# Block-diagonal tiles and runs of 1024 bytes in the token stage of a two-path attention kernel, and gradient rows that are scaled where they are used

## The chip, the cores and the metric

The kernel runs on one core of a Trainium2 chip. The metric is the device time of one execution in microseconds; the median of the runs counts. Matrix products are in bf16 with sums in f32.

## The reference

The forward function mixes two attention paths by a gate; the kernel computes its output and, for a given `grad_out`, the gradients of eleven of its inputs.

```python
def A(x, wq, wk, wv, wo):             # S=2048, D=576, 32 heads of 18, one shared k and v
    p = softmax(scores(x @ wq, x @ wk) * 18 ** -0.5)
    return heads(p @ (x @ wv)) @ wo
def B(x, mem0, Wq, Wk, Wv, Wo):       # 32 heads of 128, 64 segments of 32 tokens
    mem = mem0                        # 8 memory rows
    for s in range(64):
        h = concat([mem, x[:, 32 * s:32 * s + 32]])
        q, k, v = h @ Wq, h @ Wk, h @ Wv          # per head
        p = softmax(where(mask, q @ k.T * 128 ** -0.5, -1e9))
        o = (p @ v) @ Wo
        mem = o[:, :8]; outs.append(o[:, 8:])
    return concat(outs)
g = sigmoid((x * gate_w).sum(-1))
out = g * A(x, ...) + (1 - g) * B(x, ...)
grads = vjp(out)(grad_out)
```

Path B is the second path. Its gradient starts from the rows `(1 - g) * grad_out`, called db in the kernel, with `1 - g` in `omg_all`.

## The kernel before

The program is one sequence of stages on one core. A preparation (0 to about 111 us) projects path A's queries, transposes inputs and scales the gradient rows. Then come a projection stage for path B, the chain of segments forward (woven with path A's first pass), **the token stage** `b_bulk`, the chain backward (woven with path A's second pass), `b_post`, and the weight gradients `b_dw`.

**The token stage.** In the chain only the 8 memory rows of each segment have been attended; here the 2048 tokens of path B are. The work is 128 groups: 16 token tiles of 128 tokens (four segments of 32) by 8 groups of four heads. The loop `for t in range(NG + 9)` runs one *tick* per group, software-pipelined: `order` lists the stages of a tick with their delays in ticks, and each engine executes its part of that list in the order in which it is written. A tick holds, in this order:

- `st_QT`, `st_KT`: TensorE transposes four heads of q, then of k, into a PSUM tile `x_tr`; VectorE copies 128x512 of it to `x_qT`, `x_kT` (L836). Each *rides* one more 128x128 transpose in the fifth place of the same PSUM tile: that of the memory part of dS (with q) and of P (with k) of an older group. VectorE copies the ridden 128x128 (L822) into columns 128 to 255 of a tile `x_DT` or `x_PT`, and fills columns 0 to 127 by its own 32x32 stream transpose of the token part (L823).
- `st_OT`, `st_VT`, `st_GT`: the same for o, v and dO. ScalarE copies o (`x_oT`) and v, VectorE copies dO (`x_dOT`). GpSimd multiplies `x_prod = x_dOT * x_oT` (L938).
- `st_B`, in four parts in between: the products of o with the output weights.
- `st_Om`, `st_Qm`: one 128x512 matmul each, of the memory rows (a block-diagonal `x_vmB` or `x_kmB`) with columns 128 to 255 of `x_PT` or `x_DT`, into a PSUM tile `x_po`.
- `st_SDm`, `st_SDx`: scores and dP. ScalarE takes the exponential `x_E`; VectorE forms `x_dS` (L897).
- `st_R`, `st_M`: VectorE's row sum `x_l`, reciprocal `x_r` and mask on `x_E` (L904); GpSimd's product `x_P` (L915).
- `st_K`, every second tick: gradients of the memory rows' k and v.
- `st_Ox`, `st_Qx`: the token part of o and dq. A token attends its own segment only, so each of four heads needs four 32x32 blocks of P: `attend_x` issues 16 matmuls in 32x32 tiles of the array, which add to `x_po`. ScalarE copies the result to `x_o` or `x_dq`.

Tiles of 128x2048 (16 heads of one token tile, a *chunk* of four ticks) are loaded and stored by SP's queue: `x_q`, `x_k`, `x_v`, `x_dO` in, `x_o` and `x_dq` out, each partition in one run of 4096 bytes.

**The gradient rows.** In the preparation, a loop of 20 steps u multiplies path A's output weights and the gate-scaled rows (`product`), and beside it `scale_go` (L1739, VectorE) forms db for token tile u+1 one step ahead, GpSimd copies its last columns to `xtail` (L1846), TensorE transposes it, and every fourth step `keep_rows` (L1743) stores four tiles to `db_dram` by GpSimd's DMA queue. `put` evacuates a product to a tile `a_QDs` (L82 on VectorE, L84 on ScalarE; eight buffers) and stores it to `qs_dram` in turn by SP's and GpSimd's queues. An earlier loop of 20 steps does the same for the queries, with `scale_go` into `xtok`. In `b_post`, whose loop over t has VectorE copies `y_T` (L1405) in each step, `load_h` reads `db_dram` back at t = 31 as `w_h` for the weight gradients.

Of the kernel before, what the change touches and what calls it, by code (L numbers as in the profile page):

```python
# [51 lines left out]
class Kern:  # L52
# [52 lines left out]
    def setup_B_dram(self, dram):  # L105
# [4 lines left out]
        self.db_dram = t("db_dram", [T, D])  # L110
# [617 lines left out]
    def b_bulk(self, wp, lp, sp, psum):  # L728
# [3 lines left out]
        mB = {w: [wp.tile([P, 4, 4, E], BF16, name=f"x_{w}mB{i}") for i in range(2)] for w in ("k", "v")}  # L732
        mT = {}
        C = {}
        NG = NTT * 8
        NC = NTT * 2

        def load(c, names):
# [4 lines left out]
            for w in names:  # L743
# [12 lines left out]
                else:  # L756
                    d[w] = lp.tile([P, 16, P], BF16, name=f"x_{w}", bufs=BQ if w in deep else 3)
                    nc.sync.dma_start(d[w][:].rearrange("p h e -> p (h e)"),
                                      self.xtok[w][tt * P:(tt + 1) * P, h0 * P:h0 * P + 2048])
# [16 lines left out]
        def store(t, dst, src):  # L776
            if t % 4 == 3:
                tt, h0 = t // 8, 16 * (t // 4 % 2)
                due[1].append((dst[tt * P:(tt + 1) * P, h0 * P:h0 * P + 2048], src[:].rearrange("p h e -> p (h e)")))
# [11 lines left out]
        def transp(d, r, nm, pt):  # L791
            self.tr(pt[:, 4, :], d[:, 1, r, :].rearrange("p i t -> p (i t)"), P)
            o = sp.tile([P, 256], BF16, name=nm, bufs=2)
            return o, d[:, 0, r, :].rearrange("p i t -> p (i t)")

        def attend_m(PT, m):
            po = psum.tile([P, 4, P], F32, name="x_po", bufs=2)
            self.mm(po[:].rearrange("p i e -> p (i e)"), lhsT=PT[:, 128:256], rhs=m.rearrange("p i e -> p (i e)"),
# [3 lines left out]
        def attend_x(o, po, PT, v):  # L802
            for i in range(4):
                for c in range(4):
                    r32 = slice(32 * c, 32 * c + 32)
                    self.mm(po[r32, i, :], lhsT=PT[r32, 32 * i:32 * i + 32], rhs=v[r32, i, :],
                            start=False, stop=True, tp=(32 * c, 32 * c))
            nc.scalar.copy(o, po[:])
# [3 lines left out]
        def trans(t, w, nb, ride=None):  # L812
            pt = psum.tile([P, 5, P], BF16, name="x_tr", bufs=2)
            if 0 <= t < NG:
                tt, g, r, d = view(t)
                for i in range(4):
                    self.tr(pt[:, i, :], d[w][:, 4 * (g % 4) + i, :], P)
            o2 = ride and ride(pt)
            if 0 <= t < NG:
                trans_out(t, w, nb, pt)  # L820
            if o2:
                nc.vector.tensor_copy(o2[0][:, 128:256], pt[:, 4, :])  # L822
                nc.vector.transpose(o2[0][:, 0:128], o2[1])  # L823

        def trans_out(t, w, nb, pt):
            tt, g, r, d = view(t)
            if w == "v":
                o = chunk(t, "vT", [P, 4, 16, SEG], 2)
# [6 lines left out]
            o = sp.tile([P, 4, P], BF16, name=f"x_{w}T", bufs=nb)  # L835
            nc.vector.tensor_copy(o[:], pt[:, 0:4, :])  # L836
            sc[w + "T", t] = o

        def ride(t, nm, out):
            def put(pt):  # L840
                if 0 <= t < NG:
                    tt, g, r, d = view(t)
                    o2 = transp(d[nm], r, "x_" + out, pt)
                    sc[out, t] = o2[0]
                    return o2
# [73 lines left out]
        def st_Om(t):  # L919
            tt, g, r, d = view(t)  # L920
            sc["po", t] = attend_m(sc["PT", t], mB["v"][t // 4 % 2][:, g % 4])

        def st_Ox(t):
            tt, g, r, d = view(t)
            o = chunk(t, "o", [P, 16, P], 2)
            attend_x(o[:, r, :], sc.pop(("po", t)), sc.pop(("PT", t)), d["v"][:, r, :])
            store(t, self.xtok["o"], o)

        def st_OT(t):
            tt, g, r, d = view(t)  # L930
            pt = psum.tile([P, 5, P], BF16, name="x_tr", bufs=2)
            for i in range(4):
                self.tr(pt[:, i, :], d["o"][:, 4 * (g % 4) + i, :], P)
# [24 lines left out]
        def st_Qm(t):  # L958
            tt, g, r, d = view(t)
            sc["pq", t] = attend_m(sc["DT", t], mB["k"][t // 4 % 2][:, g % 4])  # L960

        def st_Qx(t):
            tt, g, r, d = view(t)
            dq = chunk(t, "dq", [P, 16, P], 2)
            attend_x(dq[:, r, :], sc.pop(("pq", t)), sc.pop(("DT", t)), d["k"][:, r, :])
# [4 lines left out]
        def st_K(t):  # L970
# [4 lines left out]
            for a in range(2):  # L975
                for i in range(4):
                    r32 = slice(32 * i, 32 * i + 32)
                    h = 4 * (g % 4 - 1 + a) + i
                    self.mm(pk[r32, a, 0, :], lhsT=d["dS"][:, 1, h, :], rhs=d["q"][:, h, :], tp=(0, 32 * i))
# [1403 lines left out]
```

## Time and profile before

| | |
|---|---|
| median of 3 runs | 5270.73 us (5256.26 to 5274.28) |
| profiled execution | 5275.43 us, span 5273.7 us |
| TensorE / VectorE / ScalarE / GpSimd busy | 95% / 67% / 62% / 41% of the span |
| mean granted TensorE clock | 0.988 |
| DMA over the span | 959.23 MB, 182 GB/s |
| token stage, first and last tick's start | 2045.41 and 2644.76 us |

A row of the timeline gives the start and the duration in us, the engine, the source line, the operation with output <- input, the shape, the count, and in brackets the idle time of the engine before it with what released it. PE is TensorE, PEld its weight loads, DVE VectorE, ACT ScalarE, POOL GpSimd, SP SyncE. A row of the waits gives the waiting engine, its tile and line, the releaser, then the total in us, the times and the longest. "issue" as a releaser is time in which the engine waited for nothing that the profile shows. A row of a DMA queue gives packets, MB and the time that its packets took as a share of 16 engines' time. A row of groups gives the count, the busy time and the mean of one in ns. A row of a source line or tile gives count, shortest/median/longest in ns, and the first and last start.

### The profile page before, as it was taken

What the parts mean: (1) busy time and instruction counts of PE and PEld (TensorE: products, weight loads), DVE (VectorE), ACT (ScalarE), POOL (GpSimd) and SP (SyncE); (2) the same over time, 40 slices, a digit from 0 to 9 for tenths busy, and PEclk for the clock granted to TensorE, in tenths of its full rate; (3) what the DMA queues carried; (4) which work ended last, traced back from release to release, by engine and by line L of the source; (5) the groups of instructions that cost most, each with busy time, mean ns of one, the idle gap of its engine ahead of it and who ended that gap; (6) DMA issues with size and microseconds to landing.
All of it is one profiled execution on the core that took longest, in us unless ns stands there. A gap on an engine that the chain in (4) does not pass through costs nothing. (4 is left out here: it accounts for less than half of the span.)

```text
span 5273.7 us, 216258 instructions
## 1 busy us (share of the span) xinstructions
PE 5025.2 (95%) x92973; PEld 2779.6 (53%) x93152; DVE 3526.8 (67%) x7041; ACT 3272.5 (62%) x4701; POOL 2166.9 (41%) x4164
## 2 busy tenths in 40 slices
PE   8999999999999998988889999999999999999999
PEld 5444444444444445666655555555555577754445
DVE  4348888888888887666657778788888841333332
ACT  4237888888888886555557777777777732222211
POOL 3015666665655655333323444444444421111213
PEclk9999999999999999999999999999999999999999
DMA  8855676656765456888885788878888787965654
GB/s 273 266 149 133 140 137 143 138 138 138 144 137 127 116 111 176 260 258 253 241 282 159 175 183 181 177 179 180 181 182 177 169 198 213 267 217 187 189 165 138
DMA packets 1070902, 959.23 MB, mean 182 GB/s; under 512 B 618245, under 2 KB 926413, under 8 KB 1059956
## 3 DMA queue, kind: packets, MB, share of 16 engines
q1 hardware_dynamic: 958556, 695.16, 54.7%
q0 software_dynamic: 102032, 240.46, 15.1%
q8 instruction: 728, 11.93, 1.0%
q10 hardware_dynamic: 9352, 9.77, 0.6%
q14 instruction: 234, 1.92, 0.1%
HBM read 518.26 MB, written 375.52 MB: 169 GB/s over the span
## 5 line engine op out<-in xcount | busy, mean ns | idle before, releaser
L2098 DVE TENSOR_TENSOR b_dS<-b_dP,b_E 128x512 bf16<-128x512 f32 x2048 | 1317.5, 685 | 559.9 <-PE b_dP L87 253.6
L1933 DVE TENSOR_TENSOR a_W<-a_dP,a_E 128x512 bf16<-128x512 f32 x2048 | 1313.8, 683 | 227.9 <-issue 103.6
L2047 ACT ACTIVATE b_E<-b_S 128x1024 bf16<-128x1024 f32 x1024 | 1049.2, 1025 | 608.5 <-PE b_dP L87 491.0
L1902 ACT ACTIVATE a_E<-a_S 128x1024 bf16<-128x1024 f32 x1024 | 1050.0, 1025 | 244.5 <-PE a_dP L87 163.6
L87 PE MATMUL a_acc<-a_E,l_VK 128*32 128x512 bf16 x4096 | 594.5, 385 | 7.8 <-issue 2.8
L87 PE MATMUL r_pj<-WT,r_dT 128*32 128x288 bf16 x12288 | 489.3, 290 | 8.9 <-issue 4.6
L87 PE MATMUL w_acc<-w_d,w_h 128*128 128x512 bf16 (+1 forms) x2342 | 480.0, 380 | 3.7 <-issue 1.1
L87 PEld LDWEIGHTS <-b_QS 32*128 32x128 bf16 (+1 forms) x8192 | 238.6, 91 | 439.9 <-issue 394.1
L87 PE MATMUL b_S<-b_KV,b_QS 32*128 32x512 bf16 x2048 | 404.7, 386 | 36.1 <-ACT b_E L2047 21.2
L87 PE MATMUL a_S<-a_QD,l_KV 32*128 32x512 bf16 x2048 | 398.7, 383 | 40.7 <-ACT a_E L1902 39.1
L87 PE MATMUL b_dP<-b_KV,b_QS 32*128 32x512 bf16 x2048 | 404.0, 389 | 3.1 <-DVE b_dS L2098 1.7
L87 PE MATMUL a_acc<-a_W,l_WK 128*32 128x512 bf16 x2048 | 405.5, 390 | 0.3 <-DVE a_W L1933 0.2
L87 PE MATMUL b_acc<-b_dS,b_QS 128*18 128x512 bf16 x2048 | 398.7, 384 | 1.8 <-issue 1.2
L87 PE MATMUL b_acc<-b_E,b_QS 128*18 128x512 bf16 x2048 | 397.6, 384 | 0.8 <-issue 0.8
L87 PE MATMUL a_dP<-a_QD,l_KV 32*128 32x512 bf16 x2048 | 398.2, 385 | 0.0
L87 PEld LDWEIGHTS <-hm 128*32 128x32 bf16 x7680 | 263.8, 96 | 196.8 <-issue 15.0
L87 PEld LDWEIGHTS <-r_dT 128*32 128x32 bf16 x12288 | 277.1, 96 | 135.5 <-issue 87.2
L87 PEld LDWEIGHTS <-w_h 128*128 128x128 bf16 (+1 forms) x2528 | 214.5, 100 | 245.2 <-issue 17.7
L938 POOL TENSOR_TENSOR x_prod<-x_dOT,x_oT 128x512 bf16<-128x512 bf16 x128 | 148.0, 1156 | 299.5 <-ACT x_oT L935 282.5
L87 PEld LDWEIGHTS <-l_KV 32*128 32x128 bf16 x4096 | 123.8, 91 | 250.5 <-issue 210.1
L87 PEld LDWEIGHTS <-l_WK 128*32 128x32 bf16 x2048 | 98.9, 93 | 218.7 <-issue 218.7
L87 PE MATMUL x_b<-WoN,x_oT 128*128 128x288 bf16 x1024 | 211.0, 290 | 1.2 <-issue 1.2
(475 smaller groups left out, 10114.0 us busy)
## 6 DMA issues: line engine op xcount, KB each, us to landing
b_QS<-qs_dram SPq DMA_DIRECT2D x233, 200.0 KB
dOx_dram<-p_tok SPq DMA_DIRECT2D x16, 1024.0 KB
c_vx<-vx_dram SPq DMA_DIRECT2D x64, 256.0 KB
krow_dram<-c_k POOLq DMA_DIRECT2D x64, 256.0 KB
qrow_dram<-c_q POOLq DMA_DIRECT2D x64, 256.0 KB
vrow_dram<-c_v POOLq DMA_DIRECT2D x64, 256.0 KB
x_q<-qx_dram SPq DMA_DIRECT2D x32, 512.0 KB
x_dO<-dOx_dram SPq DMA_DIRECT2D x32, 512.0 KB
```

What stands on the lines that cost most here:

```text
L87: return self.nc.tensor.matmul(out, lhsT, rhs, start=start, stop=stop, tile_position=tp, skip_group_check=True)
L938: nc.gpsimd.tensor_tensor(out=sc["prod", t][:], in0=sc["dOT", t][:], in1=oT[:], op=ALU.mult)
L1902: nc.scalar.activation(E_[n][:], S.pop(n)[:], ACT.Exp, scale=SCALEA)
L1933: nc.vector.tensor_tensor(out=W_[n][:, i, :], in0=dP[i][:], in1=E_[n][:, i, :], op=ALU.mult)
L2047: nc.scalar.activation(E_[n][:], S.pop(n)[:], ACT.Exp, scale=SCALEA)
L2098: nc.vector.tensor_tensor(out=D_[n][:, i, :], in0=dP[i][:], in1=E_[n][:, i, :], op=ALU.mult)
```

## The change

- **Token stage.** The chunk tiles become `[P, 4, 528]` with 512 of each 528 columns used, so that a partition's 4096 bytes lie in four pieces of 1024 bytes, and its DMA goes in runs of that size. The ridden transpose is copied together with q or k (128x640, one VectorE copy) and used from that tile. The stream transpose goes to a tile of its own, which is spread to a block-diagonal `[P, 4, 4, 32]` tile: for P by four VectorE copies of 32x128 into one of two tiles that are zeroed once, for dS by one GpSimd product of 128x512 with the mask `bmask`. `attend_x` then issues 4 matmuls of 128x128 instead of 16 of 32x32.
- **Gradient rows.** `db_dram` and its stores go. `load_h` reads `grad_out`, and 16 VectorE products in `b_post` (t = 32 to 47, one in each step) scale it in place.
- **Preparation.** `a_QDs` has twelve buffers instead of eight, and both loops scale two tiles ahead instead of one.

```diff
@@ -107,7 +107,6 @@
         t = lambda nm, sh, dt=BF16: dram.tile(sh, dt, name=nm)
         self.xT_dram = t("xT_dram", [NKT, P, T])
         self.dbT_dram = t("dbT_dram", [NKT, P, T])
-        self.db_dram = t("db_dram", [T, D])
         self.da_dram = t("da_dram", [T, D])
         self.dxB_dram = t("dxB_dram", [T, D])
         self.st_WoT = t("st_WoT", [4, P, J])
@@ -730,10 +729,12 @@
         NTT = self.NTT
         mx = self.maskX
         mB = {w: [wp.tile([P, 4, 4, E], BF16, name=f"x_{w}mB{i}") for i in range(2)] for w in ("k", "v")}
+        diag = [wp.tile([P, 4, 4, SEG], BF16, name=f"x_PTd{i}") for i in range(2)]
         mT = {}
         C = {}
         NG = NTT * 8
         NC = NTT * 2
+        pieces = lambda t: t[:, :, 0:512].rearrange("p g (i e) -> p g i e", e=E)
 
         def load(c, names):
             if c >= NC:
@@ -754,9 +755,10 @@
                             self.mtok[w[0]][tt * 32:(tt + 1) * 32, h0 * P:h0 * P + 2048]
                             .rearrange("r (g i e) -> r g i e", i=4, e=E)[:, :, i, :])
                 else:
-                    d[w] = lp.tile([P, 16, P], BF16, name=f"x_{w}", bufs=BQ if w in deep else 3)
-                    nc.sync.dma_start(d[w][:].rearrange("p h e -> p (h e)"),
-                                      self.xtok[w][tt * P:(tt + 1) * P, h0 * P:h0 * P + 2048])
+                    t = lp.tile([P, 4, 528], BF16, name=f"x_{w}", bufs=BQ if w in deep else 3)
+                    d[w] = pieces(t)
+                    nc.sync.dma_start(t[:, :, 0:512], self.xtok[w][tt * P:(tt + 1) * P, h0 * P:h0 * P + 2048]
+                                      .rearrange("p (g x) -> p g x", x=512))
 
         after = {4: ("vB",), 5: ("v",), 6: ("mT",), 7: ("q", "dO"), 9: ("k", "kB")}
         deep = ("q", "dO", "k")
@@ -776,7 +778,8 @@
         def store(t, dst, src):
             if t % 4 == 3:
                 tt, h0 = t // 8, 16 * (t // 4 % 2)
-                due[1].append((dst[tt * P:(tt + 1) * P, h0 * P:h0 * P + 2048], src[:].rearrange("p h e -> p (h e)")))
+                due[1].append((dst[tt * P:(tt + 1) * P, h0 * P:h0 * P + 2048].rearrange("p (g x) -> p g x", x=512),
+                               src[:, :, 0:512]))
 
         def store_pd(t, w, src):
             if t % 4 == 3:
@@ -788,23 +791,32 @@
                 (nc.scalar if end else nc.sync).dma_start(dst, src)
             due.append([])
 
-        def transp(d, r, nm, pt):
+        def transp(d, r, pt):
             self.tr(pt[:, 4, :], d[:, 1, r, :].rearrange("p i t -> p (i t)"), P)
-            o = sp.tile([P, 256], BF16, name=nm, bufs=2)
-            return o, d[:, 0, r, :].rearrange("p i t -> p (i t)")
+
+        def block_diag(d, r, t, nm):
+            o = sp.tile([P, 4, SEG], BF16, name=f"x_{nm}", bufs=2)
+            nc.vector.transpose(o[:].rearrange("p i q -> p (i q)"), d[:, 0, r, :].rearrange("p i t -> p (i t)"))
+            if nm == "PT":
+                full = diag[t % 2]
+                for c in range(4):
+                    r32 = slice(32 * c, 32 * c + 32)
+                    nc.vector.tensor_copy(full[r32, :, c, :], o[r32])
+            else:
+                full = sp.tile([P, 4, 4, SEG], BF16, name="x_DTd", bufs=2)
+                nc.gpsimd.tensor_tensor(out=full[:], in0=o[:].unsqueeze(2).to_broadcast([P, 4, 4, SEG]), op=ALU.mult,
+                                        in1=self.bmask[:, :, 0:1].unsqueeze(1).to_broadcast([P, 4, 4, SEG]))
+            sc[nm, t] = full
 
         def attend_m(PT, m):
             po = psum.tile([P, 4, P], F32, name="x_po", bufs=2)
-            self.mm(po[:].rearrange("p i e -> p (i e)"), lhsT=PT[:, 128:256], rhs=m.rearrange("p i e -> p (i e)"),
+            self.mm(po[:].rearrange("p i e -> p (i e)"), lhsT=PT, rhs=m.rearrange("p i e -> p (i e)"),
                     start=True, stop=False)
             return po
 
         def attend_x(o, po, PT, v):
             for i in range(4):
-                for c in range(4):
-                    r32 = slice(32 * c, 32 * c + 32)
-                    self.mm(po[r32, i, :], lhsT=PT[r32, 32 * i:32 * i + 32], rhs=v[r32, i, :],
-                            start=False, stop=True, tp=(32 * c, 32 * c))
+                self.mm(po[:, i, :], lhsT=PT[:, i].rearrange("p c q -> p (c q)"), rhs=v[:, i, :], start=False, stop=True)
             nc.scalar.copy(o, po[:])
 
         sc = {}
@@ -814,17 +826,12 @@
             if 0 <= t < NG:
                 tt, g, r, d = view(t)
                 for i in range(4):
-                    self.tr(pt[:, i, :], d[w][:, 4 * (g % 4) + i, :], P)
-            o2 = ride and ride(pt)
-            if 0 <= t < NG:
-                trans_out(t, w, nb, pt)
-            if o2:
-                nc.vector.tensor_copy(o2[0][:, 128:256], pt[:, 4, :])
-                nc.vector.transpose(o2[0][:, 0:128], o2[1])
-
-        def trans_out(t, w, nb, pt):
-            tt, g, r, d = view(t)
+                    self.tr(pt[:, i, :], d[w][:, g % 4, i, :], P)
+            trans_out(t, w, nb, pt, ride and ride(pt))
+
+        def trans_out(t, w, nb, pt, rode):
             if w == "v":
+                tt, g, r, d = view(t)
                 o = chunk(t, "vT", [P, 4, 16, SEG], 2)
                 nc.scalar.copy(o[:, :, r, :].rearrange("p s h t -> p h s t"),
                                pt[:, 0:4, :].rearrange("p h (s t) -> p h s t", t=SEG))
@@ -832,17 +839,21 @@
                     for c in range(4):
                         due[1].append((self.vT_dram[4 * tt + c][:, 16 * (t // 4 % 2):16 * (t // 4 % 2) + 16, :], o[:, c]))
                 return
-            o = sp.tile([P, 4, P], BF16, name=f"x_{w}T", bufs=nb)
-            nc.vector.tensor_copy(o[:], pt[:, 0:4, :])
-            sc[w + "T", t] = o
+            lo, hi = 0 if 0 <= t < NG else 4, 5 if rode else 4
+            if lo < hi:
+                o = sp.tile([P, 4 if w == "dO" else 5, P], BF16, name=f"x_{w}T", bufs=nb)
+                nc.vector.tensor_copy(o[:, lo:hi, :], pt[:, lo:hi, :])
+                if lo == 0:
+                    sc[w + "T", t] = o
+                if rode:
+                    rode(o[:, 4, :])
 
         def ride(t, nm, out):
             def put(pt):
                 if 0 <= t < NG:
                     tt, g, r, d = view(t)
-                    o2 = transp(d[nm], r, "x_" + out, pt)
-                    sc[out, t] = o2[0]
-                    return o2
+                    transp(d[nm], r, pt)
+                    return lambda o: (sc.update({(out + "m", t): o}), block_diag(d[nm], r, t, out))
             return put
 
         st_QT = lambda t: trans(t, "q", 2, ride(t - 8, "dS", "DT"))
@@ -918,19 +929,19 @@
 
         def st_Om(t):
             tt, g, r, d = view(t)
-            sc["po", t] = attend_m(sc["PT", t], mB["v"][t // 4 % 2][:, g % 4])
+            sc["po", t] = attend_m(sc.pop(("PTm", t)), mB["v"][t // 4 % 2][:, g % 4])
 
         def st_Ox(t):
             tt, g, r, d = view(t)
-            o = chunk(t, "o", [P, 16, P], 2)
-            attend_x(o[:, r, :], sc.pop(("po", t)), sc.pop(("PT", t)), d["v"][:, r, :])
+            o = chunk(t, "o", [P, 4, 528], 2)
+            attend_x(pieces(o)[:, g % 4], sc.pop(("po", t)), sc.pop(("PT", t)), d["v"][:, g % 4])
             store(t, self.xtok["o"], o)
 
         def st_OT(t):
             tt, g, r, d = view(t)
             pt = psum.tile([P, 5, P], BF16, name="x_tr", bufs=2)
             for i in range(4):
-                self.tr(pt[:, i, :], d["o"][:, 4 * (g % 4) + i, :], P)
+                self.tr(pt[:, i, :], pieces(d["o"])[:, g % 4, i, :], P)
             oT = sp.tile([P, 4, P], BF16, name="x_oT", bufs=3)
             nc.scalar.copy(oT[:], pt[:, 0:4, :])
             sc["oT", t] = oT
@@ -957,12 +968,12 @@
 
         def st_Qm(t):
             tt, g, r, d = view(t)
-            sc["pq", t] = attend_m(sc["DT", t], mB["k"][t // 4 % 2][:, g % 4])
+            sc["pq", t] = attend_m(sc.pop(("DTm", t)), mB["k"][t // 4 % 2][:, g % 4])
 
         def st_Qx(t):
             tt, g, r, d = view(t)
-            dq = chunk(t, "dq", [P, 16, P], 2)
-            attend_x(dq[:, r, :], sc.pop(("pq", t)), sc.pop(("DT", t)), d["k"][:, r, :])
+            dq = chunk(t, "dq", [P, 4, 528], 2)
+            attend_x(pieces(dq)[:, g % 4], sc.pop(("pq", t)), sc.pop(("DT", t)), d["k"][:, g % 4])
             store(t, self.xtok["dq"], dq)
             if t % 4 == 3:
                 C.pop(t // 4)
@@ -976,8 +987,8 @@
                 for i in range(4):
                     r32 = slice(32 * i, 32 * i + 32)
                     h = 4 * (g % 4 - 1 + a) + i
-                    self.mm(pk[r32, a, 0, :], lhsT=d["dS"][:, 1, h, :], rhs=d["q"][:, h, :], tp=(0, 32 * i))
-                    self.mm(pk[r32, a, 1, :], lhsT=d["P"][:, 1, h, :], rhs=d["dO"][:, h, :], tp=(0, 32 * i))
+                    self.mm(pk[r32, a, 0, :], lhsT=d["dS"][:, 1, h, :], rhs=d["q"][:, h // 4, i, :], tp=(0, 32 * i))
+                    self.mm(pk[r32, a, 1, :], lhsT=d["P"][:, 1, h, :], rhs=d["dO"][:, h // 4, i, :], tp=(0, 32 * i))
             dm = chunk(t, "dm", [P, 4, 2, P], 2)
             nc.scalar.copy(dm[:, g % 4 - 1:g % 4 + 1], pk[:])
             if t % 4 == 3:
@@ -993,6 +1004,8 @@
         done = {st_Ox: (4,), st_VT: (5,), st_SDx: (6,), st_K: (7,), st_Qx: (9,)}
         load(0, deep + ("mT", "v"))
         load(1, deep)
+        for x in diag:
+            nc.vector.memset(x[:], 0.0)
         for t in range(NG + 9):
             for n, st in order:
                 if n is None:
@@ -1450,7 +1463,10 @@
                         self.wmt = wm.tile([P, self.NM // P, 512], BF16, name="w_m0")
                     self.oh_rows(self.wmt[:, mt, :], mt, 0)
                 if n == 0 and t == 31:
-                    self.ht = self.load_h(self.db_dram, self.dm_dram, wH)
+                    self.ht = self.load_h(self.grad_out, self.dm_dram, wH)
+                if n == 1 and 32 <= t and t - 32 < self.NTT:
+                    nc.vector.tensor_scalar(out=self.ht[:, t - 32, :], in0=self.ht[:, t - 32, :],
+                                            scalar1=self.omg_all[:, t - 32:t - 31], scalar2=None, op0=ALU.mult)
                 if n == 0 and t < NG:
                     if t % 2 == 1:
                         load(t // 2 + 3, ("pd", "q", "dO"))
@@ -1786,7 +1802,7 @@
             nc.sync.dma_start(self.qs_dram[14:16, qb, :, 0:512].rearrange("n (i r) c -> n i r c", r=32)[:, 0:2, DA, :], b[NP:NP + 4, :])
 
         def put(pq, n, use, m, w, qb, k):
-            t = sp.tile([P, 512], BF16, name="a_QDs", bufs=8)
+            t = sp.tile([P, 512], BF16, name="a_QDs", bufs=12)
             self.evac(t[0:n], pq[0:n], use=use)
             rows_out(nc.sync if k % 2 == 0 else nc.gpsimd, t, m, w, qb)
 
@@ -1806,11 +1822,12 @@
 
         fin = consts()
         scale_go(xt, 0, self.g_all)
+        scale_go(xt, 1, self.g_all)
         for u in range(20):
             qb, m = u // 5, u % 5
             pq, n = product(wq, xT, qb, m)
-            if u + 1 < NTT:
-                scale_go(xt, u + 1, self.g_all)
+            if u + 2 < NTT:
+                scale_go(xt, u + 2, self.g_all)
             a = aq[qb, m] = sp.tile([P, 512], BF16, name="a_absq", bufs=10)
             nc.scalar.activation(a[0:n], pq[0:n], ACT.Abs)
             put(pq, n, "v", m, 0, qb, u)
@@ -1836,18 +1853,18 @@
             if u % 5 == 4 and u > 5:
                 bounds(u // 5 - 1)
         w_turn(4)
-        scale_go(go, 0, self.omg_all)
-        nc.gpsimd.tensor_copy(xl[:, 0], tail_in(go[:, 0, :]))
+        for v in range(2):
+            scale_go(go, v, self.omg_all)
+            nc.gpsimd.tensor_copy(xl[:, v], tail_in(go[:, v, :]))
         for u in range(20):
             qb, m = u // 5, u % 5
             pq, n = product(woT, daT, qb, m)
-            if u + 1 < NTT:
-                scale_go(go, u + 1, self.omg_all)
-                nc.gpsimd.tensor_copy(xl[:, u + 1], tail_in(go[:, u + 1, :]))
+            if u + 2 < NTT:
+                scale_go(go, u + 2, self.omg_all)
+                nc.gpsimd.tensor_copy(xl[:, u + 2], tail_in(go[:, u + 2, :]))
             put(pq, n, "vs"[u % 2], m, 1, qb, u)
             if u < NTT:
                 turn(dbT, go[:, u, :], u, GD, "s", tail(u))
-                keep_rows(self.db_dram, go, u)
             if u == 9:
                 for kt in range(NKT):
                     nc.sync.dma_start(self.dbT_dram[kt, :, 0:1024], dbT[:, kt, 0:1024])
```

## The prediction

> **What bounds the kernel now.** I read the page first: which engine is busiest over the span, and what the instruction queue moves.
>
> ```profile
> span 5273.7 us, 216258 instructions
> PE 5025.2 (95%) x92973; PEld 2779.6 (53%) x93152; DVE 3526.8 (67%) x7041; ACT 3272.5 (62%) x4701; POOL 2166.9 (41%) x4164
> q8 instruction: 728, 11.93, 1.0%
> ```
>
> TensorE is busy 95% on average, which says nothing of one stage; nearly all of the change lies in the token stage. So next come its first and its last tick in the timeline, then the waits and the DMA of the stretch 2080 to 2640 (the last row is the page's, of the whole span).
>
> ```profile
> 2045.41 0.39 PE L92 MATMUL x_tr<-identB,x_q 128*128 128x128 bf16 x4
> 2644.76 0.40 PE L92 MATMUL x_tr<-identB,x_q 128*128 128x128 bf16 x4
> PEld L92 <- DVE x_PT L822: 31.3, 104, 0.3
> PEld L92 <- DVE x_DT L822: 29.6, 95, 0.5
> PE x_po L87 <- issue: 18.2, 13, 2.8
> PE x_SD L87 <- issue: 12.2, 11, 2.6
> PE x_m L87 <- issue: 8.9, 6, 2.6
> DMA packets 116254, 140.27 MB, mean 250 GB/s; under 512 B 41117, under 2 KB 92571, under 8 KB 116116
> q1 hardware_dynamic: 115860, 138.00, 82.1%
> q1 hardware_dynamic: 958556, 695.16, 54.7%
> ```
>
> 128 ticks start between 2045.41 and 2644.76: 599.4 us over 127 steps, 4.72 us a step. Twice a tick TensorE waits about 0.3 us for the VectorE copies x_DT and x_PT. And 30 times it stands still for up to 2.8 us with no releaser ("issue"), 39.3 us in the three rows. The q8 row shows 16 KB a packet (11.93 MB by 728), 256 instructions if the 93 + 93 thousand of TensorE take 64 B each; I read these stops as waits for instructions behind data packets, a reading that no row proves. An undisturbed tick is seen in the timeline from 2584:
>
> ```profile
> 2584.41 0.41 DVE L836 COPY x_qT<-x_tr 128x512 bf16<-128x512 bf16 x1
> 2584.88 0.29 DVE L823 STREAM_TRANSPOSE x_DT<-x_dS 128x128 bf16<-128x128 bf16 x1
> 2585.50 0.58 ACT L935 COPY x_oT<-x_tr 128x512 bf16<-128x512 bf16 x1 [0.79 <-PE x_tr L92]
> 2585.55 0.28 DVE L823 STREAM_TRANSPOSE x_PT<-x_P 128x128 bf16<-128x128 bf16 x1
> 2586.23 1.16 POOL L938 TENSOR_TENSOR x_prod<-x_dOT,x_oT 128x512 bf16<-128x512 bf16 x1 [1.89 <-ACT x_oT L935]
> 2586.89 0.42 DVE L836 COPY x_dOT<-x_tr 128x512 bf16<-128x512 bf16 x1 [1.06 <-PE x_tr L92]
> 2587.63 0.40 PE L87 MATMUL x_po<-x_v,x_PT 32*32 32x128 bf16 x16
> 2587.68 0.18 DVE L913 RECIPROCAL x_r<-x_l 128x4 f32<-128x4 f32 x1
> 2587.93 0.61 POOL L915 TENSOR_TENSOR x_P<-x_E,x_r 128x256 bf16<-128x256 bf16 x1 [0.55 <-DVE x_r L913]
> 2588.41 0.42 DVE L897 SCALAR_TENSOR_TENSOR x_dS<-x_SD,x_P 128x256 bf16<-128x256 f32 x1 [0.56 <-ACT x_E L891]
> 2588.76 0.28 DVE L904 TENSOR_TENSOR x_E<-x_E,maskX 128x128 uint32<-128x128 uint32 x1
> 2588.95 0.42 DVE L836 COPY x_qT<-x_tr 128x512 bf16<-128x512 bf16 x1
> 2593.16 0.41 DVE L836 COPY x_qT<-x_tr 128x512 bf16<-128x512 bf16 x1
> ```
>
> From x_qT to x_qT it takes 4.54 us, then 4.21: 4.375 in the mean, the odd one with st_K. Of the 4.72 a step, 0.34 (44 us in all) are stops. The loop goes round TensorE and VectorE: the copies release transposes, these the score matmuls, and their exponential releases x_dS. VectorE has slack: 1.06 us ahead of x_dOT and 0.56 ahead of x_dS. GpSimd has 1.89 ahead of x_prod.
>
> **The change part by part.** *Tiled matmuls.* Sixteen 32x32 matmuls take 0.40 us (row 2587.63); four full ones of 128x128 take the same (rows of x_q). Twenty-four matmuls and as many weight loads a tick go, of the 116 that I count in a tick's code. On the path that is nothing, since TensorE waits 0.3 us for VectorE right behind; it shortens only the instruction stream, by about a fifth.
>
> *Merged copies.* 128x512 and 128x128 become one of 128x640.
>
> ```profile
> L82 DVE COPY xT<-trx x8: 471/482/490, 4.9 to 20.7; 128x640 bf16<-128x640 bf16 x8
> ```
>
> It takes 0.48. Now x_DT's stream transpose starts 0.47 behind the start of x_qT (2584.41, 2584.88); one copy, overlapping its successor by 0.07 as x_qT does (2588.41+0.42 against 2588.76), lets it start 0.41 behind. I take 0.05 for each of the two, 0.10 a tick, so a tick of 4.27 if nothing else came in.
>
> *What fills the diagonals.* Each tick gets one GpSimd product of 128x512, straight after x_DT's stream transpose and ahead of x_prod, and four VectorE copies of 32x128 behind x_PT's. The product has a twin elsewhere, r_dSB with the same mask, and the question is what the two engines do to each other:
>
> ```profile
> L281 POOL TENSOR_TENSOR r_dSB<-r_dS,bmask 128x512 bf16<-128x512 bf16 x64 | 69.3, 1083 | 0.7 <-DVE r_dS L1221 0.7
> 2583.73 0.61 POOL L915 TENSOR_TENSOR x_P<-x_E,x_r 128x256 bf16<-128x256 bf16 x1 [0.55 <-DVE x_r L913]
> 2584.12 0.37 DVE L904 TENSOR_TENSOR x_E<-x_E,maskX 128x128 uint32<-128x128 uint32 x1
> 64.21 0.64 DVE L1739 TENSOR_SCALAR gotok<-gotok,omg_all 128x576 bf16<-128x576 bf16 x2
> 64.70 0.30 POOL L1846 COPY xtail<-gotok 128x128 bf16<-128x128 bf16 x1 [0.70 <-DVE gotok L1739]
> 72.00 0.82 DVE L1739 TENSOR_SCALAR gotok<-gotok,omg_all 128x576 bf16<-128x576 bf16 x2
> 72.34 0.63 POOL L1846 COPY xtail<-gotok 128x128 bf16<-128x128 bf16 x2
> ```
>
> The mask needs 0.28 alone (2588.76, after x_P ended at 2588.54) but 0.37 when x_P runs to 2584.34: it ends 0.15 behind x_P. The two scalings take 0.64 together; at 72.00, with two GpSimd copies running among them, they take 0.82, 0.18 more. I read this as one engine waiting for the other's whole instruction, in turns. The scaling is the nearest row to the new copies: one bf16 input from SBUF, written to SBUF. (The copies from PSUM and the stream transposes show no such stretching: x_dOT takes 0.42 beside x_prod.)
>
> Now a tick, counted from the end of x_DT's stream transpose. GpSimd's product starts 0.07 later (as x_P at 2587.93 behind x_r's end at 2587.86) and ends at 0.07+1.08 = 1.15. The PT transpose ends about 0.75 (2585.83 less 2585.17, and some 0.1 for the longer copy ahead of it), so the first copy stands blocked until 1.15 and ends 0.15 later, at 1.30. x_oT is done by then: it ended at 2586.08, 0.91 in this count, and x_prod started 0.15 later, at 1.06, before the product can end. So x_prod is queued on GpSimd and goes in between the first and the second copy, as at 72.00: 1.30+1.16 = 2.46. Copies two to four follow in 0.15 and twice 0.05 to 0.2, I take 0.25 in all: 2.71. Behind them on VectorE are x_dOT, x_l, x_r (GpSimd's x_P waits for it), x_dS and the mask. From x_dOT to the end of the next x_DT transpose the rows give 2586.89 to 2588.95+0.47+0.29 = 2589.71, 2.82; less the 0.56 of waiting for x_E, which vanishes as VectorE is late, less 0.06 by the merging, plus 0.20 as x_dS then starts at x_r's end and the mask runs into x_P (x_P ends 0.68 behind x_r, the mask 0.15 later, against 0.63 unblocked): 2.40. Sum 5.11 a tick. It passes both 4.27 and the stops, since TensorE then has 0.8 us of slack each tick: 127 x 5.11 = 649, against 599.4: **+50**. If one turn in five escapes, the mean tick is 4.94 and it is +28; with copies of 0.2 it is 5.4 and +86. I take 5.05, a little under the sum because some ticks are disturbed: 641, **+42**.
>
> The Trainium skill ("SBUF — State Buffer", Who interferes with whom) has VectorE and GpSimd share one port pair as an exclusive lock, the second to issue blocked for the whole instruction, and counts copies in a two-port mode among its users; no row of this trace shows such a copy beside GpSimd. By that rule the sum is the +42 above; without it, the case below.
>
> *Runs of 1024 bytes.* x_q, x_k, x_v, x_dO, o and dq move in 512 KB transfers, six in each of 32 chunks; their descriptors become four times as many, and SP issues the same number of DMAs. The window's q1 packets took 82.1% of 16 x 560 us, 63 ns each at 1190 B; those of the whole span took 54.7% of 16 x 5273.7 us, 48 ns each at 725 B. About 28 x 6 x 128 = 21,500 of 4 KB become 86,000. If time went by bytes the share stays 82%; if each of the then 180,000 took the span's 48 ns, it is 96%. I leave the transfers at no cost, hidden beside the engines as now. What shorter packets can give is in the stops: 0 to 44 us, and nothing where the stops hide in TensorE's slack.
>
> *Gradient rows.* Four GpSimd issues and 2.36 MB go from the preparation; 16 scalings come into b_post.
>
> ```profile
> L1743 POOL DMA_DIRECT2D db_dram<-gotok x4: 801/806/822, 71.5 to 88.6; - x4
> 4384.70 0.58 SPq L1318 DMA_DIRECT2D w_h<-db_dram  x1
> 4395.05 0.75 DVE L1405 COPY y_T<-y_pt 128x512 bf16<-128x512 bf16 x2 [0.91 <-PE y_pt L92]
> 4399.65 0.76 DVE L1405 COPY y_T<-y_pt 128x512 bf16<-128x512 bf16 x2 [3.84 <-PE y_pt L92]
> ```
>
> Each scaling takes 0.36 (two that overlap by 0.08 take 0.64) and lies in the 3.84 us that VectorE idles in a b_post tick. Only the first can hurt: it waits for w_h, issued one tick before, and y_T's copies are behind it in VectorE's queue. If the 2.36 MB land by 4400 nothing moves; if they took a tick more, TensorE waits once, up to 5 us. I take +1.
>
> *Preparation.* Twelve a_QDs instead of eight, and scalings two ahead.
>
> ```profile
> PE w_ptr L92 <- ACT WoT L84: 6.9, 1, 6.9
> PEld L92 <- DVE xtok L1739: 4.9, 5, 3.1
> ```
>
> The 6.9 stands behind ScalarE, itself held at an a_QDs buffer by a store; four more buffers take it away. The 4.9 is what two-ahead can save. Between 2 and 12, I take 8: what is late next is the tail of stores, which must land anyway.
>
> Sum on the profiled time of 5275.4 (span 5273.7 and 1.7 around it): +42 +1 -8 = +35, 5310. The profile lay 4.7 over the median of the runs, 5270.7, so I forecast 5306.
>
> **The rivals.** *A, the copies are not blocked, or pass together.* The four 0.15 copies then end near 1.8, when x_dOT is due (1.72: 2586.89 less 2585.17), and the tick is 4.27. Stops shrink with a fifth fewer instructions and shorter packets: 127 x 4.27 = 542 without stops, 577 with 0.8 of them, so -57 to -22; I take -45. With -8 and +1 that is -52: about 5219, between 5202 (-57, -12) and 5253 (-22, -2, +6). For it: every copy has a slack of 1 us today, and most of the trace's copies beside GpSimd show nothing, though they come from PSUM. Against it: the rows at 72.00 and 2584.12.
>
> A page speaks to the size of this case: by the Trainium skill ("DMA: Bandwidth & Descriptors", Queues, rings and completion order) a DMA engine drains a whole packet of typically 9 to 17 descriptors before it turns to another queue's row. By it a fetch of instructions would wait no less behind four times as many short runs, and A would be at -22, not at -45; no row here separates the two.
>
> *B, my forecast:* 5306, its own range 5288 (+28, -12, +1) to 5345, which stops short of the 5361 of the dearest terms together.
>
> *C, DMA becomes the bound.* 180,000 packets over 16 engines at 50 ns are 563 us for the window's 117 ticks, 4.81 a tick, over A's 4.27: 611 for the stage, +12, and about 5276 in all, no change; at 60 ns 5.77, +133. Against it: the span's smaller packets are also the quicker ones (48 ns against 63), and the window has 18% in hand.
>
> *D, next to nothing:* half of the ticks blocked (5.05 and 4.27 mixed, 4.66) and the prep gain: 127 x 4.66 = 592, -7-7 = 5257, within the measurement's reach.
>
> **How the numbers follow.** What a measurement of this kernel can tell from no change is about 0.3%, 16 us. B 0.54 (slower), A 0.36 (faster), C 0.04 (half no change, half slower), D 0.06 (0.04 no change, 0.02 faster). B and A are of opposite signs and hold most of the chance, so the range has to span both: 5210 leaves out a fifth of A, 5335 a tenth of B.
>
> **What would show it.** B: the four copies each tick stand with a first one of about 0.5 us and a later one of over 1 us; x_prod starts between them; x_dOT loses its wait for x_tr, x_dS its wait for x_E, and the stage's ticks are near 5.05. A: copies under 0.2 us each, x_dOT still waiting for x_tr, ticks near 4.3. In both, instruction packets of the stage fall by a fifth, q1's packets rise to some 180,000 and the 6.9 ahead of w_ptr is gone. The forecast is wrong if x_prod never lies between two of the copies.

## The result, and the profile after

The changed kernel takes 5337.64 us in the median (5326.21 to 5341.1, four runs) against 5268.22 us of the kernel before, measured again beside it (5256.26 to 5274.28): a ratio of 1.0136 (95% interval 1.0118 to 1.0155), 69 us slower. The forecast was slower by 35, 5306, in a range up to 5335: the sign and the place were right, the forecast had half of the size, and the result lies above the range.

The profiled execution has a span of 5336.6 us, 62.9 more than before. From the timeline, the first and the last tick of the token stage:

```profile
2036.22 0.63 PE L92 MATMUL x_tr<-identB,x_q 128*128 128x128 bf16 x4
2715.88 0.39 PE L92 MATMUL x_tr<-identB,x_q 128*128 128x128 bf16 x4
```

The stage starts 9.2 us earlier and takes 679.7 us instead of 599.4, 5.35 a step instead of 4.72: +80. So +80 in the stage, -9 ahead of it, and -8 behind it. Of the 8, 5 lie in the backward chain, which the change does not touch: from the last tick's start to the first y_T it takes 1615 us before and 1610 after, and 1595 to 1612 in the experiments below. The 8 is no gain of the change.

One undisturbed tick of the changed kernel in rows of the timeline, VectorE and GpSimd alone, some rows left out:

```profile
2501.33 0.29 DVE L799 STREAM_TRANSPOSE x_DT<-x_dS 128x128 bf16<-128x128 bf16 x1
2501.79 1.07 POOL L807 TENSOR_TENSOR x_DTd<-x_DT,bmask 128x512 bf16<-128x512 bf16 x1 [0.94 <-DVE x_DT L799]
2501.93 0.28 DVE L799 STREAM_TRANSPOSE x_PT<-x_P 128x128 bf16<-128x128 bf16 x1
2502.25 2.17 DVE L804 COPY x_PTd<-x_PT 32x128 bf16<-32x128 bf16 x4
2502.82 1.15 POOL L949 TENSOR_TENSOR x_prod<-x_dOT,x_oT 128x512 bf16<-128x512 bf16 x1
2504.45 0.42 DVE L845 COPY x_dOT<-x_tr 128x512 bf16<-128x512 bf16 x1
2504.91 0.42 DVE L922 TENSOR_REDUCE x_l<-x_E 128x4 f32<-128x256 bf16 x1
2505.36 0.18 DVE L924 RECIPROCAL x_r<-x_l 128x4 f32<-128x4 f32 x1
2505.45 0.39 DVE L908 SCALAR_TENSOR_TENSOR x_dS<-x_SD,x_P 128x256 bf16<-128x256 f32 x1
2505.61 0.61 POOL L926 TENSOR_TENSOR x_P<-x_E,x_r 128x256 bf16<-128x256 bf16 x1 [1.64 <-DVE x_r L924]
2505.76 0.61 DVE L915 TENSOR_TENSOR x_E<-x_E,maskX 128x128 uint32<-128x128 uint32 x1
2506.70 0.29 DVE L799 STREAM_TRANSPOSE x_DT<-x_dS 128x128 bf16<-128x128 bf16 x1
2507.62 2.18 DVE L804 COPY x_PTd<-x_PT 32x128 bf16<-32x128 bf16 x4
```

Four copies of 32x128 take 2.17 us. They begin when GpSimd's product for dS is running and end 0.45 after x_prod's end (2503.97), while x_prod follows the product without a gap. The 1.06 us that VectorE waited for x_tr ahead of x_dOT is gone (x_dOT starts 0.03 behind the copies), so is x_dS's wait for x_E, and the mask, at 0.61, again ends 0.15 behind x_P. The row of line L804 in this tick (shortest/median/longest in ns) and the timeline of shorter windows tell how unequal the four are:

```profile
L804 DVE COPY x_PTd<-x_PT x4: 185/424/1101, 2502.2 to 2504.2; 32x128 bf16<-32x128 bf16 x4
2502.25 0.66 DVE L804 COPY x_PTd<-x_PT 32x128 bf16<-32x128 bf16 x1
2502.91 1.10 DVE L804 COPY x_PTd<-x_PT 32x128 bf16<-32x128 bf16 x1
2504.03 0.39 DVE L804 COPY x_PTd<-x_PT 32x128 bf16<-32x128 bf16 x2
```

The first copy takes 0.66 and ends 0.05 behind the end of the product for dS (2502.86). The second takes 1.10 and ends 0.04 behind x_prod's end. The last two pass at about 0.19 each. 112 of the stage's 128 ticks show this pattern. It is VectorE that waits: x_prod takes 1.156 in the median, as before (spans on GpSimd are rough), and starts as the product ends, without waiting for the first copy.

In the waits and in the busy times (PE, PEld, DVE, ACT, POOL, then the granted clock, DMA share, GB/s) of 2080 to 2640, VectorE is now the engine that is full:

```profile
ACT x_oT L946 <- PE x_tr L92: 196.8, 103, 2.6
POOL x_P L926 <- DVE x_r L924: 173.5, 102, 2.0
PEld L92 <- POOL x_P L926: 106.0, 98, 1.1
PE x_tr L92 <- POOL x_P L926: 84.3, 93, 1.0
2080.00:2640.00 560.00, 451.16 (x9475) 345.21 (x9473) 542.40 (x1346) 282.52 (x577) 291.24 (x316) 1.00 0.76 224
```

It is busy 542 of 560 us, blocked time included. TensorE, which before waited for VectorE's copies and stood still without a releaser, now waits for x_P. GpSimd forms x_P, and itself waits for x_r, which stands late in VectorE's queue. No row of PE with "issue" is left among the waits of this stretch.

The other signs that the prediction names are there: instruction packets (q8) fall from 107 to 74 in these 560 us, from 0.90 to 0.71 a tick, a fifth; q1's packets rise from 976 to 1550 a tick.

In the preparation and in b_post:

```profile
PE w_ptr L92 <- POOL w_tail L657: 0.6, 1, 0.6
102.48 1.24 PE L87 MATMUL p_pb<-WoT,p_x 128*128 128x512 bf16 x3 [2.48 <-DMA p_x<-dbT_dram]
4465.04 0.37 DVE L1468 TENSOR_SCALAR w_h<-w_h,omg_all 128x576 bf16<-128x576 bf16 x1 [3.45 <-DMA w_h<-dm_dram]
4465.43 0.75 DVE L1418 COPY y_T<-y_pt 128x512 bf16<-128x512 bf16 x2
```

The 6.9 us ahead of w_ptr are gone, and the next stage waits 2.5 for the dbT_dram loads instead. The first scaling in b_post waits 3.45 us for its load, and y_T behind it starts in its old rhythm.

### The profile page after: what moved, and what is told of

Same layout as the page of the kernel before. It is cut to its first block, busy times and chain, and to the rows that moved or that the text cites. A ratio compares the mean times of both kernels' runs of the same rounds, so it can differ in the third digit from the quotient of the medians.

```text
span 5336.6 us, 210825 instructions
## 1 busy us (share of the span) xinstructions
PE 5029.7 (94%) x90080; PEld 2787.7 (52%) x90080; DVE 3815.8 (72%) x7326; ACT 3266.4 (61%) x4701; POOL 2302.1 (43%) x4288
## 5 line engine op out<-in xcount | busy, mean ns | idle before, releaser
L804 DVE COPY x_PTd<-x_PT 32x128 bf16<-32x128 bf16 x512 | 269.3, 526 | 9.7
L946 ACT COPY x_oT<-x_tr 128x512 bf16<-128x512 bf16 x128 | 75.0, 586 | 240.3 <-PE x_tr L92 238.2
```

The source lines that it names most:

```text
L804: nc.vector.tensor_copy(full[r32, :, c, :], o[r32])
L946: nc.scalar.copy(oT[:], pt[:, 0:4, :])
```

## The experiments

Times are medians; ratios are to runs of the kernel before on the same chip, whose median was 5250 (e1 to e4), 5255 (e5 to e8) and 5248 us (e9 to e11). The expectations' absolute numbers count from the 5268 and 5338 above, so the ratios and the ticks decide. A difference between two experiments is taken from their ratios. Theory L is the prediction's: VectorE's copies and GpSimd's operations wait for each other's whole instruction, in turns.

**e1, the copies on ScalarE.**

```diff
-                    nc.vector.tensor_copy(full[r32, :, c, :], o[r32])
+                sc["PTo", t] = o        # and behind st_VT, four times:
+                nc.scalar.copy(diag[t % 2][r32, :, c, :], o[r32])
```

> Edit: the four copies that spread P to the diagonal go from VectorE to ScalarE, behind x_vT in its queue; GpSimd's product stays. Theory L (VectorE and GpSimd wait for each other's whole instruction, in turns): no VectorE copy is left to stand behind the two GpSimd products, the tick falls from 5.35 to 4.3 to 4.5, about 5215 to 5240 us. Rival W (VectorE is simply too full, nobody blocks it): only the copies' own time goes, 4 x 0.11 us a tick, about 5280. Rival G (GpSimd's added product makes x_prod and x_P late): GpSimd's work is the same, about 5335.

5250.14 us, 0.9993 (0.9978 to 1.0007): against the change's 1.0136 some 75 us are gone, the whole loss, with GpSimd's product still there, which leaves G (5335 is 1.013 of 5268) out. W's 5280 is 1.002, L's 5215 to 5240 0.990 to 0.995: the result lies between the two, and the mean tick is 4.73 where L had 4.3 to 4.5. But W had a copy at 0.11; at the 0.185 that it takes unblocked, W would have 4 x 0.185 x 127 = 94 us less than the change, 0.995, so this run does not tell L from W. The group of the copies shows one reason why the tick is longer than L had it: ScalarE has the work now.

```profile
L866 ACT COPY x_PTd<-x_PT 32x128 bf16<-32x128 bf16 x417 | 123.2, 295 | 10.1
```

This row of 2080 to 2580 is 1.18 us a tick, and a copy costs 0.3 here against 0.19 on VectorE. ScalarE is busy 414 of these 500 us, 290 before, and VectorE waits 13 times for ScalarE's x_bsb, 33.5 us in all against 15.7.

**e2, stream transposes straight into the diagonal tile.** VectorE keeps the work, in another kind of instruction.

```diff
-            nc.vector.transpose(o[:]..., d[:, 0, r, :]...)
-                    nc.vector.tensor_copy(full[r32, :, c, :], o[r32])
+                    nc.vector.transpose(full[r32, :, c, :], d[r32, 0, r, :])
```

> Edit: P's stream transpose writes straight into the diagonal tile, as four of 32x128, and the four copies go; everything stays on VectorE. Theory L: stream transposes have shown no stretching beside GpSimd, so nothing is blocked, though VectorE has more own work than with one transpose and four copies (4 x 0.25 against 0.28 + 4 x 0.11 us): tick 4.4 to 4.6, 5225 to 5255 us. Rival W: VectorE has 0.3 us more a tick than now, about 5375. Rival G: about 5335.

5241.13 us, 0.9982 (0.9964 to 0.9999). Four transposes stand beside the same two GpSimd operations (the first row is of line L802 over the whole run, the others are of the timeline):

```profile
L802 DVE STREAM_TRANSPOSE x_PTd<-x_P x512: 277/302/309, 2042.4 to 2639.3; 32x128 bf16<-32x128 bf16 x171
2403.14 1.07 POOL L807 TENSOR_TENSOR x_DTd<-x_DT,bmask 128x512 bf16<-128x512 bf16 x1 [1.13 <-DVE x_DT L805]
2403.27 1.23 DVE L802 STREAM_TRANSPOSE x_PTd<-x_P 32x128 bf16<-32x128 bf16 x4
2404.16 1.16 POOL L949 TENSOR_TENSOR x_prod<-x_dOT,x_oT 128x512 bf16<-128x512 bf16 x1
2404.61 0.42 DVE L845 COPY x_dOT<-x_tr 128x512 bf16<-128x512 bf16 x1
```

None of the stage's 512 transposes takes longer than 0.309 us. The four together take 1.23, which is more own work than one transpose (0.28) and four copies (4 x 0.19), and yet the tick from x_dOT at 2404.61 to the next at 2408.79 is 4.18. This tells L from W and G: the load on both engines is there, and the loss is not. The undisturbed tick is shorter than L had it, but the stage takes 595 us. TensorE's stops without a releaser, 38.8 us of 2080 to 2580 before, are down to 1.9, and new waits come in their place, which e6 to e10 follow up.

**e3, only the order on GpSimd.** The product for dS is issued behind x_prod.

> Edit: the same instructions, but GpSimd's product for dS is issued behind x_prod instead of ahead of it. Theory L: GpSimd is idle when the four copies come, up to x_prod's start, so most or all of them pass at 0.1 to 0.2 us each; if the last one is still caught behind x_prod it waits up to 1.2 us. Tick 4.4 to 4.9, 5230 to 5290 us. Rival W: VectorE's work is the same, about 5335. Rival G: x_prod comes 1 us earlier and x_P up to 1 us later, no gain, 5335 or more.

5265.08 us, 1.002 (1.0005 to 1.0035): 85% of the loss goes by the order of one instruction; W and G (1.013) are out. The four copies then lie beside x_prod alone:

```profile
2402.02 1.65 DVE L804 COPY x_PTd<-x_PT 32x128 bf16<-32x128 bf16 x4
L804 DVE COPY x_PTd<-x_PT x4: 182/185/1055, 2402.0 to 2402.6; 32x128 bf16<-32x128 bf16 x4
2402.44 1.18 POOL L952 TENSOR_TENSOR x_prod<-x_dOT,x_oT 128x512 bf16<-128x512 bf16 x1 [1.80 <-ACT x_oT L949]
2403.70 0.42 DVE L848 COPY x_dOT<-x_tr 128x512 bf16<-128x512 bf16 x1
```

Three copies pass at 0.185, the last of them issued as x_prod comes; the fourth stands behind x_prod for 1.055, and the four take 1.65 instead of 2.17. (The first row and the last two are of the timeline, the second of line L804 in this tick.) The mean tick is 4.84, in the expected 4.4 to 4.9.

**e4, the short runs alone**, in the kernel before.

> Edit: the kernel before with the runs of 1024 bytes alone. If TensorE's stops without a releaser are fetches of instructions behind 4 KB packets, most of the 44 us of stops in the token stage go: 5225 to 5245 us. If a fetch waits for a number of packets in bytes or a whole batch of them, no change: 5268. If the transfers become the bound: slower, 5280 to 5380.

5271.1 us, 1.0037 (1.0016 to 1.0057): slightly slower, and no gain from the stops. There are 31 of them in 2080 to 2580, as before; they take 30.9 us, where before has 38.8 and e5, with the same token stage, 35.9. Of the stage's 2080 to 2640:

```profile
DMA packets 180603, 139.44 MB, mean 249 GB/s; under 512 B 41472, under 2 KB 178547, under 8 KB 180467
q1 hardware_dynamic: 180211, 137.20, 82.5%
```

180,211 packets take 82.5% of 16 x 560 us, 41 ns each, where 115,860 took 82.1%: the time goes nearly by the bytes. Neither case of rival C came (50 or 60 ns), nor did the gain. The rule of the Trainium skill named in the prediction ("DMA: Bandwidth & Descriptors", Queues, rings and completion order) had foreseen no gain as the prediction read it, and this run agrees (1.0037). That section counts a packet in descriptors; that shorter runs make a packet no shorter in bytes is the prediction's own step, and no run shows it.

**e5, the preparation and the gradient rows alone.**

> Edit: the preparation's and the gradient rows' part of the change alone, with the token stage of before. From the changed kernel's profile, where the token stage starts 9.2 us earlier: 7 to 10 us below before. If the early start is given back later: no change.

5253.62 us, 1.0006 (0.9988 to 1.0023): no gain that shows. In its profile the token stage starts at 2029.7 and takes 606 us. In the ten profiles with this part it starts at 2029 to 2036, in the three without at 2038 to 2045: the early start is there in every profile, but it is not found in the time.

**e6, e2 with runs of 4096 bytes; e7, e2 without the store of x_o; e8, the kernel before without it.** e7 and e8 leave out a store that the result needs, so one weight gradient is formed from another tensor; they are for the time alone. The edit of e7 and e8:

```diff
+        self.xtok["o"] = self.xtok["dO"]
-            store(t, self.xtok["o"], o)
```

> Edit: e2_stream_diag (P's stream transposes written straight into the diagonal tile) with runs of 4096 bytes again. In e2 an undisturbed tick takes 4.28 us, yet the stage's mean is 4.69, with waits of up to 10 us for loads of x_k. Theory M (the stage's bytes set a floor, whatever the runs): the stage stays at 590 to 605 us, the time within 10 us of e2. Rival S (the four times as many short packets cost it): the stage falls to 545 to 570 us, 25 to 45 us below e2. Rival F (long packets delay the fetch of instructions): 10 to 45 us above e2, with stops without a releaser in place of the waits for loads.

5227.9 us, 0.9949 (0.9931 to 0.9967): 17 us below e2 (4 to 30 by the two intervals; the two ran on different chips), between M and S, and against F.

> Edit: e2_stream_diag without the store of x_o, 16.8 of the stage's 139 MB (the weight gradients read another tensor of the same size in its place, so the time of the other stages stays). Theory M (the stage's bytes set a floor): 12% fewer bytes bring the stage from 595 to 545 to 560 us, 35 to 50 us below e2. If the late x_k loads come from their place in SP's queue or from latency: less than 15 us below e2.

5224.71 us, 0.9942 (0.9924 to 0.996): 21 us below e2 (8 to 34), where M had 35 to 50 and its rival less than 15: M's size is out, and the rival is not.

> Edit: the kernel before without the store of x_o, the same 16.8 MB. Its undisturbed ticks give 4.375 x 127 = 556 us, its stage takes 599. Theory M: the 44 us of stops are the bytes' floor too, and 25 to 40 us go. Rival F (the stops are instruction fetches behind data packets, of which there are only an eighth fewer): 0 to 10 us go.

5234.9 us, 0.996 (0.9945 to 0.9975): 21 us below before (13 to 29); M had 25 to 40, F 0 to 10. F is out, and of M's range only the lower end lies within the interval. The stops without a releaser fall from 38.8 to 20.2 us, about what the run gains. Fewer bytes help in both, but for less than M had; the store's bytes and its hold on the buffers of x_o went together, and no run parts the two. In e2 and e7 the waits (2080 to 2580) that remain name one load; e2's row, then e7's:

```profile
PEld L92 <- DMA x_k<-kx_dram: 38.0, 15, 4.3
...
PEld L92 <- DMA x_k<-kx_dram: 28.0, 14, 4.8
```

**e9 and e10, five x_k buffers**, with 4096 and with 1024 bytes.

```diff
-bufs=BQ if w in deep else 3)
+bufs=5 if w == "k" else BQ if w in deep else 3)
```

> Edit: e6_stream_4k (stream transposes straight into the diagonal tile, runs of 4096 bytes) with five x_k buffers instead of four, each load of x_k issued a chunk (four ticks) earlier. Theory M (the stage's bytes set the pace): the waits move to another load, the time stays within 6 us of e6, 0.995 of before. Rival K (x_k is loaded too late; it is issued four ticks ahead, the other loads more): the 20 us of waits for x_k go, 12 to 22 us below e6, 0.991 to 0.993 of before.

5231.18 us, 0.9973 (0.9962 to 0.9984). The waits for x_k are gone and the time is not lower than e6's; K is out. M's "within 6 us of e6" and 0.995 missed as well: it is 13 us above (2 to 24). Two of the new ones, of 2080 to 2580:

```profile
ACT x_o L818 <- DMA ox_dram<-x_o: 15.6, 11, 2.8
ACT x_vT L834 <- DMA vT_dram<-x_vT: 14.0, 11, 2.7
```

Now stores that have not left their buffers hold ScalarE. I read this as theory M in a weaker form: in a stage whose DMA is 85% busy, the wait that is mended at one transfer comes back at another. It is argued from the waits; by their middle values M's sizes missed in each of e6 to e9.

> Edit: e2_stream_diag (the same with runs of 1024 bytes) with five x_k buffers. With the waits for x_k gone, what is left between this and e9 is the runs' length alone. If short runs cost nothing by themselves: the same as e9 within 5 us. If their greater number costs transfer time: 8 to 20 us above e9, with waits for other loads. If they spare fetch stops: 5 to 20 us below e9.

5239.49 us, 0.9982 (0.9969 to 0.9995): 8 us above e9 in the medians and 5 in the ratios, with q1 at 87.5% of 16 engines' time against 85.1% (2080 to 2580). Short runs do not save anything here; whether they cost 5 us or nothing this pair alone leaves open. But all three pairs point one way (e4 above before, e2 above e6, e10 above e9).

**e11, the changed kernel with runs of 4096 bytes.**

> Edit: the changed kernel with runs of 4096 bytes; four VectorE copies and GpSimd's product stay. Theory L (VectorE, blocked in turns, sets the tick at 5.4 us): loads and fetches hide in the others' slack, and the runs' length changes nothing: 1.011 to 1.016 of before. If short runs were part of the loss: 10 to 40 us less, 1.004 to 1.011.

5329.0 us, 1.0157 (1.0142 to 1.0173): no faster than the change itself. Where VectorE sets the tick, the length of the runs is hidden, as L had it.

## Why the prediction was right or wrong

- **The mechanism** came as forecast: the first copy stands behind the product for dS, x_prod gets in ahead of the second, the last two pass, x_dOT and x_dS lose their waits. Shown by the rows of the tick and by e1 to e3, each of which takes away one part of the collision and gives most of the loss back; e2 and e3 leave W and G out. One part came otherwise: the prediction has the engines wait for each other in turns, and GpSimd hardly waits (x_prod takes 1.156 in the median before and after, 1.182 in e3). The rule on the shared ports ("SBUF — State Buffer", Who interferes with whom, in the Trainium skill) agrees with the copies of 0.66 and 1.10 us; that the ports are what blocks, no run shows.
- **The size** failed, in the step that sums a tick. The sum was 5.11 and I took 5.05, "a little under the sum because some ticks are disturbed"; the trace has 5.37 in the tick shown (copies at 2502.25 and 2507.62) and 5.35 in the mean. Counted from the end of x_DT's transpose (2501.62):

  | | forecast | trace |
  |---|---|---|
  | product for dS starts | 0.07 | 0.17 |
  | product ends | 1.15 | 1.24 |
  | x_prod starts | 1.30 | 1.20 |
  | x_prod ends | 2.46 | 2.35 |
  | the copies end | 2.71 | 2.80 |
  | x_dOT starts | 2.71 | 2.83 |
  | the next x_DT transpose ends | 5.11 | 5.37 |

  The end of the copies came within 0.09 by luck. x_prod did not wait for the first copy, which is 0.19 less than forecast, and the rest of the copies end 0.45 behind x_prod, not 0.25, since a copy alone takes 0.19 and not 0.15 or less: +0.20. The two cancel. What is left is the product's late start, 0.03 ahead of x_dOT, and 2.54 in place of 2.40 from x_dOT to the next transpose's end. Most of this last term is that x_l no longer overlaps x_dOT: 0.46 between their starts, 0.34 before, and x_r follows as late. In all +0.26, 33 us over 127 ticks, and the shading of 0.06 another 8. Hardly a tick escaped (112 of 128 show the pattern), and when VectorE is the bound the stops hide: shading the sum downwards had no reason. The 8 us behind the stage, which nobody forecast, made the miss in the whole time smaller.
- **The stops** hide in TensorE's slack, as said for this case: no such row of PE is left.
- **Rival A** would have been wrong even without blocking. It let the stage fall to 542 to 577 us; e2, whose tick is as short as A's, has 595, e9 580. A was right that the stops shrink (38.8 us before, 1.9 in e2, 12.2 in e6, 7.1 in e9, of 2080 to 2580), and did not see that waits for transfers take their place, 32 us for x_k alone in e2. Short runs by themselves do not do it (30.9 in e4). Without the store of x_o about half of them go (20.2 in e8). Whether the others are instructions fetched late is open.
- **Rival C** was half right: when VectorE is freed, the waits that remain in e2, e7 and e9 name transfers, but their time goes mostly by the bytes (41 ns a packet in e4), little by the count.
- **Preparation:** -8 forecast, -9.2 in the stage's start; w_ptr's 6.9 went. e5, whose stage starts 16 us earlier than before's and takes 7 longer, does not find it in the whole time, within -6 to +12; it is not settled whether the token stage gives it back.
- **Gradient rows:** +1 forecast, nothing seen; the wait of 3.45 fits into the idle 3.84.
- **The matmuls:** the four of 128x128 take 0.40 us (2503.67), as the sixteen did; that they cost nothing on the path is as said, and fits e2's short tick.

The fastest whole versions are e6 and e9, which keep the 128x128 matmuls and drop the copies and the short runs. They are 0.5 and 0.3% faster than the kernel before, and 1.6 to 1.9% faster than the changed one.

## What to carry to other kernels

Before adding a short VectorE copy between SBUF tiles, look at what GpSimd has queued at that moment: a copy of 0.19 us can cost a whole GpSimd instruction, and again the next one, if a second is ready when the first ends. Another kind of instruction (here the stream transpose itself, with the strided target as its output) or one place later in GpSimd's queue may remove the loss with the same work. When a sum says that one engine becomes the bound, take the sum, and look at each of its terms, since two wrong ones can cancel. Then ask what the stage's next bound is: here the freed engine's time went in good part into waits for transfers.

## What the runs showed of the hardware that was not expected

VectorE's x_l overlaps x_dOT in some kernels (0.33 to 0.34 us between their starts, at 0.42 each) and in others not (0.44 to 0.46). It is not a matter of a late queue: the overlap is lost in nearly every tick of the changed kernel and in e2, e3, e6, e7 and e9 to e11, also where x_dOT has waited for TensorE, and it is there in before, e1, e4, e5 and e8. The first group has 32-partition instructions on VectorE ahead of x_dOT, the last of them on partitions 96 to 127; the second has none there. That this is the cause no run shows.

A GpSimd instruction holds VectorE's copies up to its end (0.66 and 1.10 us for a copy of 0.19) and hardly slows itself, and 32x128 stream transposes beside it are not stretched at all (0.277 to 0.309 us). ScalarE takes 0.295 us for a 32x128 bf16 copy that VectorE does in 0.19. And loads and stores in runs of 1024 in place of 4096 bytes, 180,211 packets in place of 115,860, cost almost the same DMA time (82.5% against 82.1%).
